# Attention over sampled blocks and an MLP on one core: one scale per pair of W_in pieces, block numbers read at once, zero rows on another queue, and another order of the work

## The chip, the cores and the metric

The kernel runs on one core of a Trainium2 chip. The metric is the device time of one execution in microseconds (us), and less is better. A core has the engines TensorE (PE in the profile, with its weight load as PEld), VectorE (DVE), ScalarE (ACT), GpSimd (POOL) and SyncE (SP). Each executes its own instructions in the order in which the program has them, and waits at an instruction until what it reads or overwrites is ready. DMA transfers are issued by an instruction on one of the engines (SPq and ACTq in the profile are the DMA-issuing instructions of SyncE and ScalarE) and then run beside it.

## The reference

```python
def _attn_ref(q, k, v, sampled_blocks):          # 4 batches, 8 heads, 768 positions, 64 wide
    scores = (1.0 / np.sqrt(D)) * np.matmul(q, k.transpose(0, 1, 3, 2))
    # mask: same or neighbouring block of 32; all rows and columns of the first and
    # the last block; and for each block of queries its 3 sampled blocks of keys
    scores = np.where(mask, scores, -1000000000.0)
    scores = scores - np.max(scores, axis=-1, keepdims=True)
    attn = np.exp(scores)
    attn = attn / (np.sum(attn, axis=-1, keepdims=True) + 1e-09)
    return np.matmul(attn, v).astype(np.float32)

def _moe_ref(x, w_in, w_out):                    # 3072 tokens, 512 -> 2048 -> 512
    h = x @ w_in
    sp = np.where(h > 20.0, h, np.log1p(np.exp(np.minimum(h, 20.0))))
    g = h * np.tanh(sp)
    return (g @ w_out).astype(np.float32)
```

The attention's output, with the heads side by side, is the MLP's input x. The two weights arrive with 64 bits to a number (8.4 MB each); everything else has 32.

## The kernel before, in words

**Number formats.** Each operand of a large product is scaled by a power of two and split into two f16 parts, a high one and the remainder, and a product is three f16 products. The scale comes from the sum of squares: a "gram" matmul of the operand with itself (L373), whose diagonal DVE adds up (L388, "diag"), a matmul with ones that adds over the partitions (L396), and three small DVE operations that make the power of two and its inverse (L407 to L409, "root").

**Weights.** W_in is worked on in 8 pieces of 256 columns (`piece_i`), W_out in 16 of 128 rows (`piece_o`). A piece is loaded into a buffer of its own kind (`wr`, of which there are 3, for W_in; `wor`, which shares the ring `raw` of 6 with q, k and v, for W_out), turned into f32 by three DVE operations (L901, L904, L907), and, for W_in, measured (gram, diag, root) and split: the high part on ACT (L962) or DVE (L964), the low part on DVE (L968). The scale of one piece of W_in is a column of `ws`; two pieces share a root, and four DVE instructions for each such pair, later than the root, make what the MLP needs of it: `scales_w` takes the larger of the two inverse scales (`gq`, L1033), its reciprocal (`rq`, L1034) and the factor `gsc` of each piece (L1035); `scales_b` then makes `hsc` (L1041). W_out has one scale in all.

**Attention.** Each batch is cut into 14 jobs (`attend`), here counted from 0. A job is a chain over the engines: scores S (L674, PE), maximum mx (L737, DVE), its negative nb (L746, ACT), the exponentials pt (L756, ACT), transposes t (L680, PE), the f16 high part ph (L779, ACT), the low part pl (for the first six jobs a product that subtracts, L787 on PE, and a copy, L792 on ACT; later L783 on DVE), the product with v into the tile obank (L818, PE), the division r and xs (L837 to L840, DVE), and transposes tx back into x, split into xh and xl (L864 to L873). The sampled keys are copied out of kt into kg, one block at a time, at an address that comes out of a register: on POOL (L611), or, for some of the early jobs, on ACT (L608), which reads the register with a `value_load` (L607) ahead of each copy. The rows of v are gathered by DMAs on SP's queue (L628 to L635, vg from vd); a duplicate among the sampled blocks reads rows of zeros behind each batch of vd, which four DMAs write at the program's start (`which`, L339 in the kernel after).

**MLP.** For each 256 tokens and each piece of W_in the h products (L1068, PE), the copy hs of a piece (L1079, ACT, scaled by gsc), the nonlinearity over a pair of pieces (L1098 to L1122), and the y products with W_out (L1162, and L1281 for the last tokens). The first 70 or so us are loads, scales and splits; from about 100 us on, the jobs of the attention and the MLP of the tokens already done run side by side.

**Order.** Every step is a task with a number, and the string `ORDER` gives the order in which the program has them. A letter behind a number puts the task on the second of its engines (for the loads of weights no letter is ACT and b is SP; for the high part of W_in no letter is ACT and b is DVE). `+n` puts n matmuls ahead of the task whose result nobody reads (`fill`, L1506, "fillers" below).

## Time and profile before

| what | value |
|---|---|
| time before, median of 3 runs | 738.99 us (736.54 to 740.02) |
| the profiled execution, its own time | 739.2 us |
| its span in the profile | 737.4 us |
| TensorE clock granted, mean over the span | 0.983 of full speed |
| PE busy | 695.9 us (94%) |
| DVE, ACT, POOL busy | 566.1, 583.0, 298.4 us |
| DMA, mean over the span | 140 GB/s |

The profiled execution's own time is 1.8 us more than its span, and 0.2 us more than the median of the runs. The profile's page cuts the span into 40 equal slices; PE is below nine tenths in the first six of them only, that is in the first 110 us.

### The profile page before, as it was taken

What the parts mean: (1) busy time and instruction counts of PE and PEld (TensorE: products, weight loads), DVE (VectorE), ACT (ScalarE), POOL (GpSimd) and SP (SyncE); (2) the same over time, 40 slices, a digit from 0 to 9 for tenths busy, and PEclk for the clock granted to TensorE, in tenths of its full rate; (3) what the DMA queues carried; (4) which work ended last, traced back from release to release, by engine and by line L of the source; (5) the groups of instructions that cost most, each with busy time, mean ns of one, the idle gap of its engine ahead of it and who ended that gap; (6) DMA issues with size and microseconds to landing.
All of it is one profiled execution on the core that took longest, in us unless ns stands there. A gap on an engine that the chain in (4) does not pass through costs nothing.

```text
span 737.4 us, 28793 instructions
## 1 busy us (share of the span) xinstructions
PE 695.9 (94%) x11758; PEld 532.9 (72%) x11758; DVE 566.1 (77%) x1139; ACT 583.0 (79%) x927; POOL 298.4 (40%) x390
## 2 busy tenths in 40 slices
PE   5667799999999999999999999999999999999997
PEld 3445588865776767776777767677776778888887
DVE  6998788898777766878868768898897685745584
ACT  3695588999987878888888889978777787777782
POOL 2120424518554463174852623674574631023101
PEclk9978899999999999999999999999999999999999
DMA  9886767652444653335336564353423563000001
GB/s 327 289 256 201 217 212 195 206 148 64 141 117 139 189 175 98 97 120 171 114 105 178 180 216 112 130 140 92 152 85 95 166 212 143 1 1 16 29 17 71
DMA packets 60041, 103.59 MB, mean 140 GB/s; under 512 B 8579, under 2 KB 20868, under 8 KB 59908
## 3 DMA queue, kind: packets, MB, share of 16 engines
q1 hardware_dynamic: 59568, 100.96, 44.3%
q8 instruction: 92, 1.51, 0.9%
q10 hardware_dynamic: 340, 0.79, 0.3%
q14 instruction: 41, 0.34, 0.1%
HBM read 84.58 MB, written 17.14 MB: 138 GB/s over the span
## 4 chain that ended last, share of the span: by engine, by line
PE 79%; DVE 8%; DMA 7%; ACT 2%; issue 1%; SPq 1%; ACTq 0%; DVEq 0%
PE h_None L1068 30%; PE y L1162 21%; PE yr L1281 9%; PE t L680 6%; PE obank L818 5%; PE s L674 5%; DMA wor<-in_moe_w_out_dram 2%; DMA raw_k<-in_k_dram 2%; DMA vg<-vd 2%; PE obank L1281 1%; PE tx L680 1%; DVE mx L737 1%; DVE wo L904 1%; DMA raw_v<-in_v_dram 1%; DVE pl L783 1%
## 5 line engine op out<-in xcount | busy, mean ns | idle before, releaser
L1068 PEld LDWEIGHTS <-wi 128*128 128x128 f16 x2304 | 223.7, 98 | 35.2 <-issue 1.6
L1068 PE MATMUL h_None<-xh,wi 128*128 128x256 f16 x1152 | 207.1, 273 | 0.0
L611 POOL COPY kg<-kt 128x256 f16 x246 | 115.5, 504 | 154.6 <-PE s L674 128.2
L1162 PE MATMUL y<-wo,g 128*128 128x512 f16 x672 | 160.6, 379 | 0.0
L1068 PE MATMUL h_None<-xl,wi 128*128 128x256 f16 x576 | 157.3, 273 | 0.4 <-DVE xl L867 0.4
L1162 PEld LDWEIGHTS <-g 128*128 128x128 f16 x768 | 73.5, 98 | 68.5 <-issue 0.6
L756 ACT ACTIVATE pt<-s,nb,ns 128x256 f32<-128x256 f32 (+1 forms) x208 | 106.9, 582 | 0.7
L1120 POOL TENSOR_TENSOR g<-hs_None,g 128x1024 f16<-128x1024 f32 x33 | 73.3, 2223 | 72.4 <-ACT g L1114 54.5
L783 DVE SCALAR_TENSOR_TENSOR pl<-t,ph 128x512 f16<-128x512 f32 x99 | 67.0, 685 | 31.2 <-ACT ph L779 30.8
L779 ACT ACTIVATE ph<-t 128x512 f16<-128x512 f32 x112 | 66.0, 598 | 30.9 <-PE t L680 30.5
L1079 ACT ACTIVATE hs_None<-h_None,gsc 128x512 f32<-128x512 f32 x96 | 65.6, 688 | 20.8 <-PE h_None L1068 18.4
L1107 DVE SCALAR_TENSOR_TENSOR hs_None<-us_None,hs_None 128x1024 f32<-128x1024 f32 x48 | 59.6, 1241 | 24.4 <-ACT us_None L1106 24.3
L680 PE MATMUL t<-ident,pt 128*128 128x128 f32 x448 | 69.1, 284 | 7.6 <-ACT pt L756 4.7
L1068 PE MATMUL h_None<-xr,wi 128*128 128x256 f16 x576 | 68.6, 273 | 0.0
L680 PEld LDWEIGHTS t<-ident,pt 128*128 128x128 f32 x448 | 54.7, 147 | 18.5 <-issue 5.6
L737 DVE TENSOR_REDUCE mx<-s 128x4 f32<-128x1024 f32 x44 | 53.6, 1219 | 16.0 <-PE s L674 15.8
L1098 ACT ACTIVATE us_None<-hs_None,hsc 128x1024 f32<-128x1024 f32 x48 | 55.2, 1149 | 4.1 <-DVE sg L1148 2.9
L1103 POOL TENSOR_TENSOR us_None<-us_None 128x1024 f32<-128x1024 f32 x16 | 33.0, 2062 | 54.7 <-DVE us_None L1101 48.8
L818 PEld LDWEIGHTS <-ph 128*32 128x32 f16 x2408 | 43.4, 97 | 14.7 <-issue 10.0
L1106 ACT ACTIVATE us_None<-us_None 128x1024 f32<-128x1024 f32 x48 | 50.7, 1058 | 0.3
L1105 ACT ACTIVATE us_None<-us_None 128x1024 f32<-128x1024 f32 x48 | 50.6, 1057 | 0.3
L818 PE MATMUL obank<-vg,ph 128*32 128x129 f16 (+2 forms) x2168 | 46.1, 211 | 3.4 <-DMA vg<-vd 3.2
(262 smaller groups left out, 1238.8 us busy)
## 6 DMA issues: line engine op xcount, KB each, us to landing
vg<-vd SPq DMA_DIRECT2D x320, 65.0 KB, 2.4
vg<-vd SPq DMA_DIRECT2D x80, 195.0 KB, 3.0
wr<-in_moe_w_in_dram SPq DMA_DIRECT2D x8, 1024.0 KB, 8.1
wor<-in_moe_w_out_dram SPq DMA_DIRECT2D x15, 512.0 KB, 4.5
vd<-v SPq DMA_DIRECT2D x12, 520.0 KB, 4.4
vg<-vd SPq DMA_DIRECT2D x12, 520.0 KB, 4.4
raw_k<-in_k_dram SPq DMA_DIRECT2D x12, 512.0 KB, 6.8
raw_q<-in_q_dram SPq DMA_DIRECT2D x12, 512.0 KB, 4.6
```

The source lines that it names most:

```text
L611: nc.gpsimd.tensor_copy(out=dst, in_=tl["kt", b][:, :, ds(j, BS)])
L680: nc.tensor.matmul(out, src, ident, start=start, stop=stop, is_transpose=True)
L737: nc.vector.tensor_reduce(out=mx.rearrange("p g w -> p (g w)"), in_=tl[ks].rearrange("p g (w k) -> p (g w) k", k=KT), axis=AX.X, op=ALU.max)
L756: ex = lambda o, x, g, w: nc.scalar.activation(out=o, in_=x, func=AF.Exp, bias=nb[:, g, w:w + 1], scale=tl["ns", b, sus[w]["qb"] // TB][:, ...
L779: nc.scalar.activation(out=new(at_, "ph", ("ph", i, j), [P, 2, 2, P], F16), in_=tl["t", i, j], func=AF.Copy, scale=PSC)
L783: nc.vector.scalar_tensor_tensor(out=new(at_, "pl", ("pl", i, j), [P, 2, 2, P], F16), in0=tl["t", i, j], scalar=PSC, in1=tl["ph", i, j], o ...
L818: nc.tensor.matmul(obank[cs, at:at + v1 - v0], p[:, k, g, cs], vt[:, k, 2 * c + g, v0:v1], start=j == 0 and g == 0 and k == 0 and n == 0, ...
L1068: nc.tensor.matmul(h[:, f2, 0:n].rearrange("p (s q) -> p s q", q=BS), wi[:, fp, w, cc, fs], x[:, s0:s0 + sn, cc], start=f2 == 0 and k == 0 ...
L1079: nc.scalar.activation(out=tl[kq][:, 2 * (fp % 2):2 * (fp % 2) + 2, 0:n], in_=tl[kh][:, :, 0:n], func=AF.Copy, scale=gsc[:, fp:fp + 1])
L1120: add("POOL", 2.3 * c, lambda: nc.gpsimd.tensor_tensor(out=g(1), in0=hs(), in1=g(0), op=ALU.subtract), r=[kq, ("gh",) + kp], w=[kp], use=[kg],
L1162: nc.tensor.matmul(tl[ky], tl["g", b, t, k][:, g, f, q], wo_at(fc)[:, w], start=fc == 0 and n == 0, stop=fc == NFC - 1 and n == 2)
L1281: nc.tensor.matmul(R(i), lhs, rhs, start=head and j == n == 0, stop=k == NFC // 4 - 1 and j == 1 and n == 2, skip_group_check=True)
```

## The change

Four things change.

- Two pieces of W_in that follow one another (a quad, four times 128 columns) get one scale. Their grams add into one PSUM tile, one diag and one root of a single column follow, and the root writes its inverse straight into `gq`. `scales_w` goes, and so do `iv_i`, `gsc` and `rq`; the copy hs is scaled by a constant.
- The block numbers of the gathers that ACT does are read into registers by one instruction at the program's start, behind the operations that make them, where before each of 18 was read by an instruction of its own ahead of its copy. 30 numbers are read; ACT has 21 of the copies now.
- The four DMAs that write the rows of zeros go to SP's queue, in a task of their own (`zero_rows`), where before ACT issued them right behind the memset.
- `ORDER` is another one. Among what moves: 42 fillers where there were 24, and at other places; 12 of the 24 loads of weights are issued by ACT (pieces 2, 4, 6 and 7 of W_in, and 8 of the 16 of W_out) where one was; the high parts of two pieces of W_in are made by DVE; the order of the small DVE operations.

```diff
-    iv_i = const.tile([P, NFP], F32, name="iv_i")
-    gsc, gq, rq, sco = (const.tile([P, n], F32, name=name) for n, name in ((NFP, "gsc"), (NFC // 4, "gq"), (NFC // 4, "rq"), (NFC // 4, "sco")))
+    gq, sco = (const.tile([P, NFC // 4], F32, name=name) for name in ("gq", "sco"))
...
+        tl["zeros"] = z
+        early.extend(su["qb"] * NR + r for job in jobs for su in job["sus"] if su["early"] and not job["dense"] for r in range(NR))
+        regs["act"] = nc.values_load_multi_w_load_instructions(
+            offk[0:1, early[0]:early[-1] + 1], [mybir.EngineType.Activation], min_val=0, max_val=S - BS,
+            skip_runtime_bounds_check_because="a sampled block is one of NB")[1]
+
+    def zero_rows():
         for b in range(B):
-            nc.scalar.dma_start(out=vd[b][S:S + BS].rearrange("s h d -> s (h d)"), in_=z)
-
+            nc.sync.dma_start(out=vd[b][S:S + BS].rearrange("s h d -> s (h d)"), in_=tl["zeros"])
...
-                    j = nc.scalar.value_load(offk[0:1, k:k + 1], min_val=0, max_val=S - BS)
+                    j = regs["act"][k - early[0]]
...
-        add_gram(("wi", k), [lambda: a0_i(k)], [key], "h", ss, [ks], [("wq", ks)] if k == k0 else (), cls)
...
-            add_root(kp, lambda: tl[ks], lambda: root(kp, new(sb, "ws", ksc, [P, 2]), iv_i[:, k0:k + 1]),
+            add_gram(("wi", k0), [lambda n=n: a0_i(n) for n in (k0, k)], [("wi", k0), key], "h",
+                     lambda: new(sb, "wq", ks, [P, 1]), [ks], [("wq", ks)], cls)
+            add_root(kp, lambda: tl[ks], lambda: root(kp, new(sb, "ws", ksc, [P, 1]), gq[:, k0 // 2:k0 // 2 + 1]),
                      [ks], [], [ksc, ("iv", k0)], [("ws", ksc)], cls)
...
-        sc = lambda: tl[("ws", k0)][:, k - k0:k - k0 + 1]
+        sc = lambda: tl[("ws", k0)]
...
-    def scales_w(k):
-        def fn():
-            nc.vector.tensor_reduce(out=gq[:, k:k + 1], in_=iv_i[:, 2 * k:2 * k + 2], axis=AX.X, op=ALU.max)
-            nc.vector.reciprocal(out=rq[:, k:k + 1], in_=gq[:, k:k + 1])
-            nc.vector.tensor_scalar(out=gsc[:, 2 * k:2 * k + 2], in0=iv_i[:, 2 * k:2 * k + 2], scalar1=rq[:, k:k + 1], scalar2=-2.0 * GSC, op0=ALU.mult, op1=ALU.mult)
-        add("DVE", 0.7, fn, r=[("iv", 2 * k)], w=[("gs", k)], key=-3)
...
-                                 scale=gsc[:, fp:fp + 1])
+                                 scale=-2.0 * GSC)
...
+    add("SP", 2.0, zero_rows, r=["off"], w=["z"], use=[("z",)], key=9, lat=2.5, kind=("dma", 1.2, B))
...
-    any(scales_w(k) for k in range(NFC // 4))
...
 ORDER = """
-    7 0 1 2 3 8+3 4 9 6 5 10 76 11 12 52 13 14 117b 18 93b 15 54 16 28+2 19 92 22 62 20 17 84 23 99b 29 24 68 67 30 21
+    7 0 1 2 3 5 4 6 9+3 10 115b 11 12 13+1 14 15 19 16 20 23 17 92 29+4 98b 21 18 62 24 30+1 25 80 73 31 22 54 74 26
```

Where a scale is made, DVE's rows change as follows, for the first two pieces of W_in (`wr` is a piece as it was loaded, `gram_wi` its gram, `tp_w` the root's tile). Before, from the diag of the one piece to the end of their common root:

```order
L388 SCALAR_TENSOR_TENSOR gram_wi_785,wq_851<-gram_wi_785,ident 128x128
L907 SCALAR_TENSOR_TENSOR wi<-wr_305,wi 128x1024
L737 TENSOR_REDUCE mx_984<-s_604 128x4
L901 TENSOR_SCALAR wi<-wr_585 128x1024
L837 TENSOR_SCALAR r_1018<-obank 128x2
L838 RECIPROCAL r_1018<-r_1018 128x2
L840 TENSOR_TENSOR xs_1019<-obank,r_1018 128x128
L388 SCALAR_TENSOR_TENSOR gram_wi_986,wq_851<-gram_wi_986,ident 128x128
L904 SCALAR_TENSOR_TENSOR wi<-wr_585,wi 128x1024
L407 TENSOR_SCALAR tp_w_1032<-tp_w_1032 128x2
L408 TENSOR_SCALAR iv_i<-tp_w_1032 128x2
L409 TENSOR_SCALAR ws_1050<-tp_w_1032 128x2
```

In the kernel after, from the last operation on piece 0 as loaded (`wr_383`), over the one diag for both pieces, to the root; `wr_597` is the next piece:

```order
L907 SCALAR_TENSOR_TENSOR wi<-wr_383,wi 128x1024
L737 TENSOR_REDUCE mx_796<-s_624 128x4
L907 SCALAR_TENSOR_TENSOR wi<-wr_305,wi 128x1024
L901 TENSOR_SCALAR wi<-wr_597 128x1024
L388 SCALAR_TENSOR_TENSOR gram_wi_800,wq_996<-gram_wi_800,ident 128x128
L904 SCALAR_TENSOR_TENSOR wi<-wr_597,wi 128x1024
L837 TENSOR_SCALAR r_1014<-obank 128x2
L838 RECIPROCAL r_1014<-r_1014 128x2
L840 TENSOR_TENSOR xs_1015<-obank,r_1014 128x128
L907 SCALAR_TENSOR_TENSOR wi<-wr_597,wi 128x1024
L407 TENSOR_SCALAR tp_w_1001<-tp_w_1001 128x1
L408 TENSOR_SCALAR gq<-tp_w_1001 128x1
```

One diag stands where two did, and the root is one column wide and writes `gq`. Behind these rows follow the root's last operation (L409), the high part of piece 0, now made by DVE (L964), and the first operation on piece 6 (L901), which is loaded into the buffer that the first of these rows gives free.

On DVE, ahead of the maximum of job 6 (`mx<-s`), with the last pieces of W_in and the first of W_out (`wor`) in work. Before:

```order
L901 TENSOR_SCALAR wo<-wor_2383 128x512
L968 SCALAR_TENSOR_TENSOR wi<-wi,ws_2245 128x1024
L901 TENSOR_SCALAR wo<-wor_2548 128x512
L904 SCALAR_TENSOR_TENSOR wo<-wor_2383,wo 128x512
L1041 TENSOR_SCALAR hsc<-gq,iv_x 128x1
L904 SCALAR_TENSOR_TENSOR wo<-wor_2548,wo 128x512
L737 TENSOR_REDUCE mx_2859<-s_2702 128x4
```

After:

```order
L840 TENSOR_TENSOR xs_2517<-obank,r_2516 128x256
L901 TENSOR_SCALAR wo<-wor_2271 128x512
L1041 TENSOR_SCALAR hsc<-gq,iv_x 128x1
L904 SCALAR_TENSOR_TENSOR wo<-wor_2271,wo 128x512
L907 SCALAR_TENSOR_TENSOR wo<-wor_1511,wo 128x512
L968 SCALAR_TENSOR_TENSOR wi<-wi,ws_2136 128x1024
L1041 TENSOR_SCALAR hsc<-gq,iv_x 128x1
L737 TENSOR_REDUCE mx_2689<-s_2562 128x4
```

Before, the decode of two pieces of W_out is begun in the stretch ahead of the maximum (two L901); after, of one.

On ACT, around the small operation nb of the same job, with the low parts pl of the job before it. Before:

```order
L779 ACTIVATE ph_1_2853<-t_1_2803 128x512
L746 ACTIVATE nb_2876<-mx_2859,ns_1_1282 128x4
L792 ACTIVATE pl_0_2878<-t_0_2644 128x512
L792 ACTIVATE pl_1_2880<-t_1_2803 128x512
L756 ACTIVATE pt_2930<-s_2702,nb_2876,ns_1_1282 128x256 x4
```

After:

```order
L779 ACTIVATE ph_1_2691<-t_1_2664 128x512
L792 ACTIVATE pl_0_2693<-t_0_2521 128x512
L962 ACTIVATE wi<-wi,ws_2049 128x1024
L746 ACTIVATE nb_2711<-mx_2689,ns_1_1284 128x4
L792 ACTIVATE pl_1_2761<-t_1_2664 128x512
```

Both low parts of the earlier job stand behind nb before; after, the first of them stands ahead of it.

## Rows read from the trace of the kernel before

**Rows 1.** Busy time by stretch: us, PE, PEld, DVE, ACT, POOL, PEclk, DMA share, GB/s.

```profile
0.00:20.00 20.00, 10.81 (x92) 7.98 (x100) 11.97 (x43) 7.48 (x9) 6.50 (x19) 1.00 0.94 332
20.00:70.00 50.00, 32.56 (x955) 24.39 (x939) 47.78 (x91) 37.21 (x74) 7.22 (x11) 0.86 0.80 246
70.00:100.00 30.00, 23.67 (x640) 18.78 (x639) 22.49 (x51) 17.34 (x34) 9.97 (x16) 0.83 0.69 207
...
140.00:700.00 560.00, 557.10 (x8858) 418.87 (x8856) 421.73 (x849) 465.37 (x733) 254.44 (x329) 1.00 0.40 123
```

**Rows 2.** DVE's groups, 15 to 130 us, shapes apart: busy us, mean ns, idle before.

```profile
L904 DVE SCALAR_TENSOR_TENSOR wo<-wor,wo 128x512 int32<-128x512 int32 x13 | 11.3, 883 | 0.0
...
L907 DVE SCALAR_TENSOR_TENSOR wo<-wor,wo 128x512 int32<-128x512 int32 x13 | 9.3, 721 | 0.0
L968 DVE SCALAR_TENSOR_TENSOR wi<-wi,ws 128x1024 f16<-128x1024 f32 x7 | 8.9, 1276 | 0.0
L904 DVE SCALAR_TENSOR_TENSOR wi<-wr,wi 128x1024 int32<-128x1024 int32 x7 | 8.5, 1220 | 0.0
...
L901 DVE TENSOR_SCALAR wo<-wor 128x512 int32<-128x512 int32 x15 | 6.8, 456 | 4.5 <-DMA wor<-in_moe_w_out_dram 4.5
...
L901 DVE TENSOR_SCALAR wi<-wr 128x1024 int32<-128x1024 int32 x7 | 5.0, 714 | 0.4 <-DMA wr<-in_moe_w_in_dram 0.4
...
L840 DVE TENSOR_TENSOR xs<-obank,r 128x256 f32<-128x256 f32 x8 | 3.4, 425 | 0.3
L1035 DVE TENSOR_SCALAR gsc<-iv_i,rq 128x2 f32<-128x2 f32 x4 | 2.8, 699 | 0.1
...
L388 DVE SCALAR_TENSOR_TENSOR gram_wi<-gram_wi,ident 128x128 f32<-128x128 f32 x8 | 2.3, 290 | 0.0
...
L1034 DVE RECIPROCAL rq<-gq 128x1 f32<-128x1 f32 x4 | 0.7, 164 | 0.1
...
L1033 DVE TENSOR_REDUCE gq<-iv_i 128x1 f32<-128x2 f32 x4 | 0.6, 144 | 0.0
```

**Rows 3.** DVE's timeline between the maxima of jobs 5 and 6.

```profile
77.73 1.23 DVE L737 TENSOR_REDUCE mx<-s 128x4 f32<-128x1024 f32 x1 [1.47 <-PE s L674]
78.87 0.15 DVE L1033 TENSOR_REDUCE gq<-iv_i 128x1 f32<-128x2 f32 x1
...
80.90 0.15 DVE L1033 TENSOR_REDUCE gq<-iv_i 128x1 f32<-128x2 f32 x1
...
86.30 0.45 DVE L901 TENSOR_SCALAR wo<-wor 128x512 int32<-128x512 int32 x1 [2.04 <-DMA wor<-in_moe_w_out_dram]
...
90.00 1.21 DVE L737 TENSOR_REDUCE mx<-s 128x4 f32<-128x1024 f32 x1
```

**Rows 4.** ACT's timeline around nb of job 6.

```profile
91.25 0.30 ACT L746 ACTIVATE nb<-mx,ns 128x4 f32<-128x4 f32 x1 [4.83 <-DVE mx L737]
91.46 1.06 ACT L792 ACTIVATE pl<-t 128x512 f16<-128x512 f32 x2
```

**Rows 5.** PE's timeline: three fillers, and the next product of job 5 with v.

```profile
58.48 0.81 PE L1506 MATMUL obank<-neg 128*128 128x240 f16 x3
...
92.09 0.25 PE L818 MATMUL obank<-vg,pl 128*32 128x65 f16 x4 [3.18 <-ACT pl L792]
```

**Rows 6.** SP's timeline, 86 to 93 us: start, us until issued.

```profile
86.73 5.77 SPq L893 DMA_DIRECT2D wor<-in_moe_w_out_dram  x3
92.70 0.33 SPq L628 DMA_DIRECT2D vg<-vd  x1
```

**Rows 7.** DMA issues by group: KB each, median us from issue to landing.

```profile
wr<-in_moe_w_in_dram SPq DMA_DIRECT2D x8, 1024.0 KB, 8.1
...
vd<-z ACTq DMA_DIRECT2D x4, 65.0 KB, 5.5
```

**Rows 8.** Waits of all engines: us in total, times, longest.

```profile
ACT kg L608 <- issue: 2.9, 9, 0.9
```

**Rows 9.** Issues at L893: ns min/median/max, first and last start us.

```profile
L893 SPq DMA_DIRECT2D wor<-in_moe_w_out_dram x15: 327/382/1650, 50.4 to 127.8; - x15
```

More of the change, by code (lines that the diff above doesn't have):

```diff
@@ L572, in globals_v @@
         add("SP", 0.9, fn, r=VD3(b), w=[("vg", n)], key=-1, lat=2.3, kind=("dma", 0.5, 2))
-    regs = {}
+    regs, early = {}, []
     def block_at(eng, name, table, k, hi):
@@ L1013, in fn @@
             nc.vector.tensor_tensor(out=gox, in0=gmx, in1=iv_o, op=ALU.mult)
-        add_root(kp, lambda: tl["am", "wo"], fn, [("am", "wo")], [("gs", k) for k in range(NFC // 4)], ["sc_o"], (), cls - 2)
+        add_root(kp, lambda: tl["am", "wo"], fn, [("am", "wo")], [("iv", k) for k in range(0, NFP, 2)], ["sc_o"], (), cls - 2)
     def parts_o(fc, cls):
@@ L1042, in scales_b @@
                 out=hsc[:, b, ks], in0=gq[:, ks], scalar1=iv_x[:, b:b + 1], scalar2=-0.5 * float(2.0 ** -26) / GSC,
-                op0=ALU.mult, op1=ALU.mult), r=[("gs", k) for k in ks] + [("sc", "v", b, 0)], w=[("hsc", b, k)], key=-3)
+                op0=ALU.mult, op1=ALU.mult), r=[("iv", 2 * k) for k in ks] + [("sc", "v", b, 0)], w=[("hsc", b, k)], key=-3)
         add("DVE", 0.2, lambda: nc.vector.tensor_scalar(
@@ L1079, in hs_fn @@
             nc.scalar.activation(out=tl[kq][:, 2 * (fp % 2):2 * (fp % 2) + 2, 0:n], in_=tl[kh][:, :, 0:n], func=AF.Copy,
-                                 scale=gsc[:, fp:fp + 1])
-        add("ACT", 0.72 if part is None else 0.45, hs_fn, r=[kh, ("gs", fp // 2)], w=[("hsw", b, t, fp, part)],
+                                 scale=-2.0 * GSC)
+        add("ACT", 0.72 if part is None else 0.45, hs_fn, r=[kh], w=[("hsw", b, t, fp, part)],
             new=[("hs", kq)] if fp % 2 == 0 else (), use=[kq], key=-4)
@@ L1380, in attn_mish_kernel @@
         load(0, "v", [j], "us" if j < 2 else "hs")
-    add("ACT", 1.0, lambda: which(new), w=["off", "z"],
-        new=[("hs", ("z",))], key=-9, lat=6.0, kind=("dma", 0.9, 2 + B))
+    add("ACT", 1.0, lambda: which(new), w=["off"],
+        new=[("hs", ("z",))], key=-9, lat=6.0, kind=("dma", 0.9, 2))
+    add("SP", 2.0, zero_rows, r=["off"], w=["z"], use=[("z",)], key=9, lat=2.5, kind=("dma", 1.2, B))
     for j in T3:
@@ L1665 @@
[L1665 to L1667 removed]
+    7 0 1 2 3 5 4 6 9+3 10 115b 11 12 13+1 14 15 19 16 20 23 17 92 29+4 98b 21 18 62 24 30+1 25 80 73 31 22 54 74 26
+    94b 58 28 32 81 33 116 163 198b 56 27 34 52 39 35 43 40 196 188 164 75 36 60 68 117 165 166 37 167 118 38 70 176
@@ new lines @@
+    1512 2218 1479 1513 1528 1460 2231 1489 1480 1531 1514 1515 2236 2167 1461 2200b 1497 2333 1481 2232 1482 1516
+    1532 2237 2201 1529 1620 2334 2202 2229 2233 2203 1534 2335 1501 1579 2238 2336b 1483 1517 1530 1502 2230 1518
+    2239 1535 1520 2254 2219 2337 1536 1521 2327 2240 1537 2255 1511 2220 1519 2204b 1522 2234 1538 1578 1503 1508
+    2259 1504 2205 2241b 1505 1542 2242 2235 1576 1543 1575 1539 1544 2260 1540 2221 1541 2250 2243 2256 1553 2244
+    2222 1523 1554 2251 1533 1524 1555 2275 2252b 1556 2247 2276 1550 1557 2257 2223 1561 2226 1581 1562 2261 1545
@@ L1668 @@
+    2676 2642b 2679 2643 2674 2678 2685 2644 2681 2645b 2682 2690 2692b 2673 2686 2688 2693 2689 2695 2680 2696 2683
+    2697 2699 2698 2687 2691 2694 2700 2701
 """
```

201 lines of the change are left out of this document (95 added, 106 removed), and 17 rows, old and new, of the table ORDER.

## The prediction, made before the kernel ran

> **What bounds the kernel now.** I read first the busy time by stretch, since the change works on the weights and the first jobs only [rows 1]. From 140 to 700 us PE is busy for 557.1 of 560 us, at full clock; there the kernel waits for nothing but PE's own work, which the change leaves as it is. What PE loses it loses early: it is idle for 9.2 us of the first 20, for 17.4 of the 50 that follow, and for 6.3 between 70 and 100, together 32.9 us. A time saved here moves the whole rest forward, if PE gets its work sooner by it.
>
> Next I ask which engine sets the pace in each of these stretches. Between 20 and 70 us it is DVE, with 47.78 of 50 us busy, where ACT has 37.21 and POOL 7.22 [rows 1]. So what DVE is spared there counts nearly whole, and what another engine is spared counts nothing. Between 70 and 100 us no engine is full (DVE 22.49 of 30), so the timelines of the engines have to tell. They show one large hole, and a chain of waits through four engines. DVE begins the maximum of job 5 at 77.73 and that of job 6 only at 90.00, 12.27 us later, with 2.04 us of waiting for a load of W_out in between [rows 3]. ACT stands 4.83 us at nb of job 6 for that maximum, and the two low parts pl of job 5, which need nothing of it, stand behind nb in ACT's order [rows 4]. PE waits 3.18 us for the first of them at 92.09 [rows 5]. On SP three loads of W_out take 5.77 us to issue, from 86.73, and a gather of v stands behind them until 92.70 [rows 6]; 15 loads there have a median of 0.382 us, so three of them without a wait are 1.15, and 4.6 us are a wait for buffers [rows 9].
>
> **The change, part by part.** The sum is made against the profiled execution's own time, 739.2 us, which is 0.2 above the median of the three runs.
>
> *The scale.* Four of eight diags go, at 0.29 us each: 1.2 us. The twelve instructions of the four scale groups go: 0.6, 0.7 and 2.8 us, together 4.1 [rows 2]. I count half of these groups, 2.05 us, in DVE's full stretch, and leave the other half to the next part, since two of the groups begin, with L1033, between the two maxima [rows 3]. Against that, DVE takes over the high parts of two pieces of W_in from ACT. The trace has no such operation on DVE. The nearest rows are the first step of the decode, one input of the same 128x1024 (0.714), and the low part, two inputs and the same output (1.276) [rows 2]; I take the first, as it too is a scalar operation on one input, and get 1.4 for both, 2.55 at most. So DVE's full stretch gets 1.2 + 2.05 - 1.4 = 1.85 us shorter. The bounds: 3.9 if all four groups lay in it (1.2 + 4.1 - 1.4), and 0.6 if the high parts take 2.55 and the factor's operation L1035, whose 0.699 is far above the 0.164 of its neighbour L1034 of a like size [rows 2], had mostly been a wait: the groups are then 12 x 0.16 = 1.9, half of it 0.95, and 1.2 + 0.95 - 2.55 is even -0.4. I keep +0.4 us as the worst end.
>
> *The order between the maxima.* After the change DVE has between the two maxima, by the rows' means: the maximum 1.22 [rows 3], twice 0.456 and 0.883 and 0.721 for the decode of W_out, a diag 0.29, a low part 1.276, an xs 0.425, and about ten small operations of 0.17: 9.0 us, with no second load of W_out to wait for [rows 2]. So job 6 gets its maximum 3.3 us earlier than the 12.27 of before, and pl of job 5 no longer waits for it, since the first stands ahead of nb. What PE gains by that is its own wait there, 3.18 us [rows 5]; I take 3.2, and 0 as the other end, where PE then waits for the next thing (the gather of v behind SP's loads, or job 6 itself).
>
> *The buffers of W_in.* There are three, so piece 6 is loaded into the one that the last operation on piece 0 frees. A load takes 8.1 us from issue to landing [rows 7], and its issue 0.38 [rows 9]: 8.5. From that operation to the first on piece 6, DVE has by the new order four operations of 1.22 (a maximum, two last steps of a decode, taken at the middle step's time, and one middle step), two of 0.71, a diag of 0.29, an xs of at most 0.43 and five small ones of 0.16: 7.8 us [rows 2, 3]. So where before DVE waited 0.4 us for W_in in all [rows 2], it now waits 0.7 for this piece; 0 if a few of those operations are held up themselves, 1.4 if piece 7 comes as late.
>
> *Edits that I cost at nothing.* The 18 reads of a register on ACT: the profile's row for what they left before a copy is 2.9 us in nine gaps [rows 8], and ACT has 12.8 us to spare in the 50 where DVE has 2.2 [rows 1]; if that cover is gone, they are worth the 2.9. Twelve loads issued by ACT instead of one cost it 11 x 0.38 = 4.2 us [rows 9], under the same cover. The zero rows: 0.26 MB leave the first 20 us, in which the transfers run at 332 GB/s with the engines 0.94 busy [rows 1, 7]; that is 0.8 us of transfer, which may bring what comes behind forward by as much, or nothing if the loads wait for DVE anyway; the four issues take SP 4 x 0.38 = 1.5 us at about 30 us [rows 9], and the first gathers of v stand behind them. I take nothing for both, with -0.8 and +1.5 as ends. The 18 more fillers take 0.27 us each (0.81 for three [rows 5]), 4.9 in all; PE has 32.9 us of idle time in the first 100 us, where they stand [rows 1], so nothing.
>
> The sum: 739.2 - 1.85 - 3.2 + 0.7 = 734.85, say **734.8 us**, by 4.4 us or 0.6% faster. All good ends together (3.9, 3.2, 0 for the buffers, 0.8, 2.9) give 728.4; all bad ends (+0.4, 0, +1.4, +1.5) give 742.5.
>
> One rule of the Trainium skill speaks against half of this. Much of the second part hangs on loads of W_out that come in time, and the row is SP's 5.77 us for three issues, with a gather behind them [rows 6]. The page "DMA: Bandwidth & Descriptors", section "Issuing engines are not separate DMA queues", says that DMAs started by different engines share the same transfer engines, and that starting them from several engines saves only the time that it takes to start them. By the row the gain is the gather's 4.6 us of standing in line; by the rule the loads themselves land no sooner for being issued on ACT.
>
> **The rivals.** *The loads still come late* (about the same time). The mechanism is the one just told: DVE's 2.04 us of waiting for W_out [rows 3] stays, wherever it then stands, and the part between the maxima brings 3.2 - 2.0 = 1.2. The sum is then 739.2 - 1.85 - 1.2 + 0.7 = **736.9**. For it speaks that 70 to 100 us moves 207 GB/s with a DMA share of 0.69, below the 332 of the start, so that it is not the transfer alone that limits [rows 1], but a buffer; against it that the gather no longer stands behind.
>
> *The gain is hidden*: PE's holes are filled by another wait of the same length, since each job's chain passes DVE and ACT in turn, and the 1.85 of DVE's are given back to W_in pieces (1.4 of 1.85). The time is 739.2 - 0.5 - 0 = **738.7**.
>
> *The clock* (faster still). PE's granted clock is 0.86 between 20 and 70 us and 0.83 between 70 and 100, and 1.00 before and from 140 us on [rows 1]; with its two levels, 2.4 and 1.2 GHz, that is 0.28 x 50 + 0.34 x 30 = 24 us at half. More fillers at other places could end this. If the 10 us at half in the second stretch went, where PE is busy for 0.79 of the time, PE would be spared 10 x 0.79 / 2 = 4.0 us, and the time is **730.8**. Against it: there PE waits for others, and its steps are a part of the chain only. The page "TensorE: Matmul & The Clock Gate", Part 1, says that the clock is throttled by default and that activity of the engine releases it; these rows agree, with 1.00 in the stretch where PE is over 0.9 busy, though the first 20 us have it too, with PE busy for 10.81.
>
> *ACT stands in its own way* (slower). ACT now issues eight loads of W_out into the ring of six that q, k and v share. An issue that finds no free buffer holds up every operation behind it: nb, pt, ph, and with them DVE and PE. The price of one such wait is what SP's row shows, 4.6 us [rows 6, 9]. One of them on the chain makes the gain nothing (734.8 + 4.6 = 739.4); the case is slower than before by 0.5% from 8.1 us of such waits on; two of them give 734.8 + 9.2 = **744.0**. For it speaks that ACT is the engine through which each job's chain passes three times; against it that SP waited there in a stretch where ACT had 12.7 us free, so that a well placed issue costs nothing [rows 1].
>
> **How the numbers follow.** The sum as worked out: 0.41. The clock besides: 0.10. Loads late: 0.21. Gain hidden: 0.14. ACT blocked: 0.14. A difference of 0.5%, 3.7 us, is about what a measurement of this kernel can tell from none, so faster is below 735.3 and slower above 742.7. The sum's own range, 732 to 737, lies on both sides of 735.3; I count three fifths of it, 0.25, as surely faster, half of the rest (0.08) too, and with the clock and a part of the late loads (0.07, as the other terms may be at their good ends) that makes 0.50. ACT blocked gives 0.12 slower, the rest of it the same; what is left, 0.38, is the same. The predicted time is 734.8; the range is 728.4 to 742.5, the ends of the bounds, with the slower rival outside.
>
> **What would show it.** Right: no L1033 to L1035 on DVE, four diags; PE idle between 20 and 70 us down from 17.4 by about 2 and between 70 and 100 from 6.3 to about 3; 140 us to the end unchanged; the wait of nb of job 6 below 2 us. Wrong: DVE rows that wait for wr by more than 2 us; ACT's issues L893 of over 1 us with PE or DVE waiting for ACT behind them; the high parts L964 over 1.3 us; PE's granted clock at 0.95 or more before 100 us, which would be the clock's rival; or PE idle in the steady part, where I expect nothing.

## The result, and the profile after

The changed kernel takes 746.44 us (median of 4 runs, 745.63 to 747.72) where the kernel before took 739.44 (4 runs). The ratio is 1.0118, with a 95% interval from 1.0084 to 1.0152: it is slower, by 1.2%, which is 8.7 us by the ratio (the medians alone are 7.0 apart), and outside of the range forecast. The profiled execution took 745.63, its span is 743.9.

The busy time by stretch has the columns of [rows 1]:

```profile
0.00:20.00 20.00, 11.50 (x119) 8.57 (x119) 12.21 (x44) 7.64 (x10) 6.79 (x19) 0.95 0.95 328
20.00:70.00 50.00, 28.55 (x662) 21.10 (x647) 37.82 (x61) 26.10 (x56) 4.47 (x5) 0.64 0.76 230
70.00:100.00 30.00, 26.11 (x822) 20.33 (x821) 26.32 (x61) 22.45 (x48) 11.99 (x17) 0.95 0.82 233
...
140.00:700.00 560.00, 553.25 (x8822) 414.62 (x8820) 435.48 (x866) 449.57 (x722) 246.58 (x313) 1.00 0.41 123
700.00:743.90 43.90, 40.04 (x367) 35.58 (x364) 26.72 (x41) 26.56 (x29) 10.80 (x8) 1.00 0.08 31
```

Against [rows 1], three numbers stand out. Between 20 and 70 us every engine does less: DVE is busy for 37.82 us instead of 47.78, ACT for 26.10 instead of 37.21, PE for 28.55 instead of 32.56. None of them is full any more, so they wait for one another. PE's granted clock is 0.64 there instead of 0.86 (that the clock is not the cause is shown below, at the two halves of the order). And PE is idle for 6.75 us between 140 and 700 us, where it was idle for 2.90. Only the stretch from 70 to 100 us went as forecast: PE is idle for 3.9 us instead of 6.3.

What stops the engines is in ACT's timeline of the changed kernel. An ACTq row is the issue of a load, and the wait in brackets is printed at the operation behind it:

```profile
34.89 0.40 ACTq L893 DMA_DIRECT2D wr<-in_moe_w_in_dram  x1
35.34 0.60 ACT L792 ACTIVATE pl<-t 128x512 f16<-128x512 f32 x1 [3.78 <-DMA vd<-z]
35.84 0.29 ACT L746 ACTIVATE nb<-mx,ns 128x4 f32<-128x4 f32 x1
...
48.62 0.37 ACTq L893 DMA_DIRECT2D wr<-in_moe_w_in_dram  x1
49.11 1.02 ACT L608 ACTIVATE kg<-kt 128x256 f16 x3 [6.07 <-DMA vg<-vd]
...
55.46 0.37 ACTq L893 DMA_DIRECT2D wr<-in_moe_w_in_dram  x1
55.88 0.30 ACT L746 ACTIVATE nb<-mx,ns 128x4 f32<-128x4 f32 x1 [3.47 <-DMA vg<-vd]
```

Three times ACT comes to a load of W_in, cannot issue it, and everything behind stands: 3.78, 6.07 and 3.47 us, 13.3 in all. The releaser is neither PE nor DVE, and not the buffer either. It is a transfer that has nothing to do with W_in, issued by SP: a gather of v for the second and the third, and for the first, by the profile, a zero row. The program shows why. DMAs signal their end by one of eight semaphores, DMAHW0 to DMAHW7, in turn, and an issue waits for the earlier one that had its own. These are the first and the second of the three in ACT's order, with what each waits for:

```
29 L893 DMA wr_798<-in_moe_w_in_dram 128x4x512 [waits DMAHW3_49,DMAHW0_49,DVE_49]
42 L893 DMA wr_1093<-in_moe_w_in_dram 128x4x512 [waits DMAHW6_49,DMAHW5_49,DVE_49]
```

Of the two semaphores of the first, DMAHW3 is that of the load that filled the buffer before (piece 0), and DMAHW0 is its own. Its own had last gone to the third store of v, and not to a zero row: the four zero rows have DMAHW1 to DMAHW4. On SP the stores stand right ahead of the zero rows:

```profile
24.23 7.92 SPq L553 DMA_DIRECT2D vd<-v  x3
32.20 2.24 SPq L339 DMA_DIRECT2D vd<-z  x4
```

The third store is issued at 31.8; the trace's semaphore signals have its last one at 34.83, 0.06 us ahead of ACT's issue at 34.89, and the last ones of the four zero rows at 35.05 to 35.76, behind it. So the name of the releaser in the profile's row is wrong here, and the store of v is what ACT waited for. For the second and the third, the last signals of their semaphores come at 48.55 and 55.36, and are those of gathers of v.

DVE is the buffer's last reader, and had been done: its last operation on the buffer of the first, the first row below, ended at 32.29, 2.6 us ahead of the issue. So ACT's work was tied to SP's transfers. (ACT's load of piece 2 at 25.32, ahead of the three, is another matter: it waited 1.23 us for its buffer, until DVE's last operation on piece 3.) DVE's timeline shows what follows:

```profile
31.07 1.22 DVE L907 SCALAR_TENSOR_TENSOR wi<-wr,wi 128x1024 int32<-128x1024 int32 x1
32.21 1.22 DVE L737 TENSOR_REDUCE mx<-s 128x4 f32<-128x1024 f32 x1
...
51.95 0.30 DVE L388 SCALAR_TENSOR_TENSOR gram_q<-gram_q,ident 128x128 f32<-128x128 f32 x1 [5.46 <-PE gram_q L373]
...
53.69 1.21 DVE L737 TENSOR_REDUCE mx<-s 128x4 f32<-128x1024 f32 x1
...
83.50 1.21 DVE L737 TENSOR_REDUCE mx<-s 128x4 f32<-128x1024 f32 x1
...
92.43 1.22 DVE L737 TENSOR_REDUCE mx<-s 128x4 f32<-128x1024 f32 x1 [0.73 <-PE s L674]
```

DVE's wait of 5.46 us leads back to ACT: the gram for which it waits stands in PE's order behind scores that wait for the copies kg of ACT's second stop (49.11 above).

```profile
50.18 0.34 PE L674 MATMUL s<-kg,q 64*32 64x160 f16 x8 [4.19 <-ACT kg L608]
```

The maxima of jobs 1 and 2 in DVE's timeline of the kernel before:

```profile
34.45 1.22 DVE L737 TENSOR_REDUCE mx<-s 128x4 f32<-128x1024 f32 x1
...
43.23 1.22 DVE L737 TENSOR_REDUCE mx<-s 128x4 f32<-128x1024 f32 x1
```

That of job 1 comes at 32.21 now, 2.2 us earlier. That of job 2 comes at 53.69, 10.5 us later; by job 6 it is 2.4 us later (92.43 for 90.00). From job 5 to job 6 it is 83.50 to 92.43, 8.9 us, where I had worked out 9.0 and the kernel before took 12.27 [rows 3].

### The profile page after: what moved, and what is told of

The parts are those of the page before. It is cut to its first block, busy times and chain, and to the rows that moved or that the text cites. A ratio compares the mean times of both kernels' runs of the same rounds, so it can differ in the third digit from the quotient of the medians.

```text
span 743.9 us, 28756 instructions
## 1 busy us (share of the span) xinstructions
PE 698.3 (94%) x11780; PEld 533.7 (72%) x11780; DVE 576.3 (77%) x1132; ACT 569.2 (77%) x924; POOL 296.5 (40%) x380
## 4 chain that ended last, share of the span: by engine, by line
PE 83%; DVE 9%; DMA 4%; issue 2%; SPq 2%; ACT 1%; ACTq 0%; DVEq 0%
PE h_None L1068 31%; PE y L1162 22%; PE yr L1281 8%; PE t L680 6%; PE s L674 5%; PE obank L818 5%; DMA vg<-vd 2%; PE tx L680 1%; PE obank L1281 1%; DMA wr<-in_moe_w_in_dram 1%; DMA raw_k<-in_k_dram 1%; DVE mx L737 1%; DVE wo L904 1%; SPq L580 1%; DVE wo L907 1%
## 5 line engine op out<-in xcount | busy, mean ns | idle before, releaser
L611 POOL COPY kg<-kt 128x256 f16 x243 | 111.8, 493 | 162.7 <-PE s L674 151.3
L1120 POOL TENSOR_TENSOR g<-hs_None,g 128x1024 f16<-128x1024 f32 x37 | 81.8, 2214 | 91.9 <-ACT g L1114 43.1
L1079 ACT ACTIVATE hs_None<-h_None 128x512 f32<-128x512 f32 x96 | 56.7, 594 | 23.5 <-PE h_None L1068 22.4
L1107 DVE SCALAR_TENSOR_TENSOR hs_None<-us_None,hs_None 128x1024 f32<-128x1024 f32 x48 | 63.3, 1319 | 8.2 <-ACT us_None L1106 8.2
L1103 POOL TENSOR_TENSOR us_None<-us_None 128x1024 f32<-128x1024 f32 x18 | 37.1, 2065 | 74.9 <-DVE us_None L1101 70.6
L674 PEld LDWEIGHTS <-q 64*32 64x32 f16 x2976 | 34.2, 94 | 22.3 <-issue 18.1
```

The costliest lines, as they stand in the source:

```text
L611: nc.gpsimd.tensor_copy(out=dst, in_=tl["kt", b][:, :, ds(j, BS)])
L674: nc.tensor.matmul(s[g][i * BS:(i + 1) * BS, c0 + cs.start:c0 + cs.stop], q[gs, c * NPR + i, qs], src[gs, a * NPR + i, ks], start=first an ...
L1107: add("DVE", 1.32 * c, lambda: nc.vector.scalar_tensor_tensor(out=hs(), in0=us(), scalar=-0.5, in1=hs(), op0=ALU.add, op1=ALU.mult), r=[ku ...
L1120: add("POOL", 2.3 * c, lambda: nc.gpsimd.tensor_tensor(out=g(1), in0=hs(), in1=g(0), op=ALU.subtract), r=[kq, ("gh",) + kp], w=[kp], use=[kg],
```

## The experiments

The runs of the kernel before that stand beside them have medians of 738.3 to 738.5 us. A difference in us is worked out from the ratios and 738.5, if nothing else is said; differences of the medians can be 1 us or so away from it.

**The loads back on SP.** All twelve loads that ACT issues, by the letter b:

```diff
-... 111 ... 145 ... 128 ... 149 ...        (pieces 2, 6, 4, 7 of W_in; W_out likewise)
+... 111b ... 145b ... 128b ... 149b ...
```

> The changed kernel with all twelve loads of weights that ACT issues put back on SP's queue, at the same places of the order. Theory A (ACT is held up): three issues of W_in loads on ACT wait 3.8, 6.1 and 3.5 us, in the trace of the changed kernel, for the end of another transfer on SP's queue, and pl, kg and nb stand behind them; without them the first jobs come earlier, PE idle between 20 and 70 us falls from 21.5 to 17 or less, and the time falls by 4 to 7 us, to 739.5 to 742.5. Theory B (the loads wait for buffers or for the transfers, whoever issues them): DVE then waits for W_in instead, and the time stays at 744 to 748.

743.59 us, 1.0093 (1.0060 to 1.0126, 4 runs). The three waits of ACT are gone and PE is idle for 16.5 us between 20 and 70, as theory A said; the time fell by 1.8 us only (2.9 by the medians), short of the 4 that it asked for, and the interval overlaps that of the changed kernel. A part of what theory B said is there as well: DVE, which waits for no load of W_in between 20 and 70 us in the changed kernel, now waits 2.78 us for the one that SP issues behind the zero rows. PE stayed idle for 6.85 us between 140 and 700.

**The code without the order.** The three edits with the order of before; `zero_rows` behind the third store of v.

> The three edits of the code (one scale per pair of pieces, one register load, zero rows on SP's queue behind the third store of v) with the order of before. Theory A: the edits do no harm, the order does; DVE is spared 1 to 4 us in its full stretch and the time is 735.5 to 739. Theory C (one scale makes both pieces of a pair wait for the later one, and the zero rows hold up SP): 741 or more.

740.27 us, 1.0030 (1.0003 to 1.0056). Neither theory as it stood: the edits do not gain, and cost little. The trace has one wait that is new, on SP and then on DVE. SP's timeline:

```profile
30.48 3.26 SPq L339 DMA_DIRECT2D vd<-z  x4
34.48 0.40 SPq L893 DMA_DIRECT2D wr<-in_moe_w_in_dram  x1
```

and DVE's:

```profile
42.26 0.69 DVE L901 TENSOR_SCALAR wi<-wr 128x1024 int32<-128x1024 int32 x1 [3.08 <-DMA wr<-in_moe_w_in_dram]
```

The same load and the same wait in SP's and DVE's timelines of the kernel before:

```profile
32.08 0.38 SPq L893 DMA_DIRECT2D wr<-in_moe_w_in_dram  x1
```

```profile
40.08 0.69 DVE L901 TENSOR_SCALAR wi<-wr 128x1024 int32<-128x1024 int32 x1 [0.41 <-DMA wr<-in_moe_w_in_dram]
```

The four zero rows keep SP for 3.26 us; the load of W_in behind them is issued at 34.48 instead of 32.08, and DVE waits 3.08 us for it instead of 0.41.

**The two halves of the order.** The code of after with the orders joined at the maximum of job 9.

```diff
-ORDER = after
+ORDER = after up to the maximum of job 9, then what is left in the order of before
```

> The code of after, with its order up to the maximum of job 9 (some 120 us) and the order of before from there on. Theory A with a second part (the later order loses 3.9 us by itself, as PE is idle for 6.75 us between 140 and 700 us where it was 2.90): 742 to 743.5. Theory D (all of the loss comes from the first 120 us, and the later gaps follow from it): 745 to 747.

748.61 us, 1.0156 (1.0125 to 1.0187).

> The code of after, with the order of before up to the maximum of job 9 and the order of after from there on. Theory A with its second part: the time of the code alone plus about 3.9, 740 to 743. Theory D: the same as the code alone, 736 to 739.

740.51 us, 1.0028 (0.9999 to 1.0057). The first lies above both ranges. The second lies in the range that I had written for theory A, 740 to 743, but that was meant as the time of the code alone plus 3.9; the code alone took 740.27, and this run the same, which is theory D. So the second part that I had given theory A falls: the later order costs nothing that can be measured, all is lost by what stands in the first 120 us. That PE is idle for 6.65 us between 140 and 700 in the first of the two, with the later order of before, says that those gaps as well are set by the early part. How an early part can do that was open here.

The first of the two also settles a rival, that the lower clock made the changed kernel slow. Its granted clock is 0.86 between 20 and 70 us, as in the kernel before, where the changed kernel had 0.64, and its profiled execution takes 748.06.

**The scale and the register load, without the zero rows' move.**

```diff
-    add("SP", 2.0, zero_rows, ...)
+            nc.scalar.dma_start(out=vd[b][S:S + BS]..., in_=z)      # in which(), as before
```

> The code with one scale and one register load, in the order of before, and with the zero rows issued by ACT at the start as before. In the run with all three edits SP took 3.26 us for the four zero-row issues, the fourth load of W_in behind them was issued at 34.48 instead of 32.08, and DVE waited 3.08 us for it instead of 0.41. Theory Z (the zero rows on SP cost what the scale spares): the wait goes back to about 0.4 and the time is 736 to 738. Theory Y (the scale gains nothing by itself, as DVE's time is not what sets the first jobs): 739 to 741, like the run with all three edits.

740.66 us, 1.0012 (0.9986 to 1.0039): theory Y by its time. DVE's wait for the fourth load is 1.54 us, over half of the way back to 0.41, and the trace has a cause that neither theory had. The scale of k is there at 11.09, by DVE's timeline,

```profile
10.94 0.15 DVE L407 TENSOR_SCALAR sc_k<-tp_k 128x1 int32<-128x1 int32 x1
```

and ACT takes it up at 11.85 only, by its own:

```profile
11.85 3.23 ACT L498 ACTIVATE kt<-raw_k,sc_k 128x1024 f16<-128x1024 f32 x3 [9.82 <-DMA raw_v<-in_v_dram]
```

In the changed kernel and the runs that have the register load and the zero rows on SP it begins at 10.25 to 10.61, and its wait ends with its scale. So the one register load delays nothing only when the zero rows do not stand ahead of it on ACT; with them, ACT begins 0.8 us late here.

**The zero rows alone**, in the kernel before.

```diff
-            nc.scalar.dma_start(out=vd[b][S:S + BS]..., in_=z)
+            nc.sync.dma_start(out=vd[b][S:S + BS]..., in_=tl["zeros"])
...
+    add("SP", 2.0, zero_rows, r=["off"], w=["z"], ...)
```

> The kernel before with one edit alone: the zero rows issued by SP behind the third store of v. Theory Z: DVE's wait for the fourth load of W_in grows to about 3 us and the time is 2 to 3 us longer, 740.5 to 742. Theory Y: 738 to 739.5.

740.19 us, 1.0027 (1.0000 to 1.0054), and DVE's wait is 2.67 us. The wait is that of theory Z; the time, 2.0 us longer, is at the low end of what it said, and the interval just touches none. With the scale and the register load besides, it was 1.0030: these two gave nothing back.

**The zero rows back on ACT**, in the changed kernel.

```diff
-            nc.sync.dma_start(out=vd[b][S:S + BS]..., in_=tl["zeros"])
+            nc.scalar.dma_start(out=vd[b][S:S + BS]..., in_=z)
```

> The changed kernel with the zero rows issued by ACT at the start again. In the changed kernel the second of ACT's W_in loads (piece 6) stands 3.78 us for a zero-row transfer. Theory A (ACT is held up by transfers on SP's queue): that wait shrinks, the two behind it (6.07 and 3.47, for gathers of v) may stay or move; the time falls by 1 to 4 us, to 742.5 to 745.5. Theory B (the loads wait for buffers): 746 to 748.

747.16 us, 1.0111 (1.0071 to 1.0150): no gain, and by the number theory B. ACT's waits are now 1.22, 4.33 and 6.04 us, 11.6 in all instead of 13.3. The first of them is for DVE, the last reader of the buffer, as theory B said; the other two are for gathers of v. The expectation rested on the profile's name for the releaser: the 3.78 us had been for the third store of v, and what moved the wait is that the semaphores go to the DMAs in turn, so that the load of piece 6 now shares one with the first store. And the run has a loss of its own, since the register load stands behind the zero rows on ACT again: ACT takes up the scale of k at 12.01, 1.28 us after it is there. So this run does not decide between the theories; the next one does.

**The four loads of W_in alone back on SP.**

```diff
-... 111 ... 145 ... 128 ... 149 ...        (pieces 2, 6, 4, 7 of W_in; W_out stays)
+... 111b ... 145b ... 128b ... 149b ...
```

> The changed kernel with the four loads of W_in alone put back on SP's queue; the eight loads of W_out stay on ACT. Theory A: the three waits of ACT go, and the time is that of the run with all twelve loads on SP, 742 to 745. The rival (the W_out loads on ACT are what holds up): 746 to 748.

742.86 us, 1.0053 (1.0030 to 1.0076), 4.8 us less than the changed kernel (3.6 by the medians), with an interval clear of its own. The three waits are gone. These four loads are the largest cause. The eight of W_out are not free of such waits: in this run two of them stand for a gather of v, by ACT's timeline,

```profile
60.84 0.36 ACTq L893 DMA_DIRECT2D wor<-in_moe_w_out_dram  x1
61.25 0.60 ACT L779 ACTIVATE ph<-t 128x512 f16<-128x512 f32 x1 [3.13 <-DMA vg<-vd]
...
81.62 0.33 ACTq L893 DMA_DIRECT2D wor<-in_moe_w_out_dram  x1
82.00 0.60 ACT L792 ACTIVATE pl<-t 128x512 f16<-128x512 f32 x1 [3.50 <-DMA vg<-vd]
```

but moving them to SP as well (1.0093, the run with all twelve there) was no faster.

**Fewer fillers besides.** 22 of them left out of that kernel.

```diff
-153+8 ... 119+4 ... 405+4 ... 346+3 ... 355+3
+153 ... 119 ... 405 ... 346 ... 355
```

> The changed kernel with the four loads of W_in on SP's queue and 22 of its 46 fillers left out, so that it has as many as the kernel before. With the loads on SP alone it stood at 1.0053 of before, and PE was idle for 6.8 us between 140 and 700 us where the kernel before was for 2.9; five of the gaps there lie right behind a 16 KB transfer of PE's own instructions, one in the kernel before. Theory F (44 more PE instructions shift where each stretch of instructions ends, and PE waits for the next one at other places): the gaps go with the fillers, PE is idle for 3 to 4.5 us there, and the time is 1.000 to 1.003 of before. Theory G (the rest of the loss is the order's, and the fillers helped the clock): 1.005 or more.

741.65 us, 1.0046 (1.0022 to 1.0071). The waits of PE between 140 and 700 us (total, times, longest) are, with 46 fillers in the run ahead of this one,

```profile
PE obank L818 <- DMA vg<-vd: 2.0, 1, 2.0
PE h_None L1068 <- issue: 1.9, 2, 1.1
PE obank L818 <- issue: 1.4, 1, 1.4
```

and with 24

```profile
PE obank L818 <- DMA vg<-vd: 3.3, 1, 3.3
PE t L680 <- DVE pl L783: 0.7, 1, 0.7
```

All that PE spent waiting on "issue", that is for nothing that the profile shows, went with the fillers, as theory F said. A wait for a gather of v grew by 1.3 us, so that PE is idle for 4.64 us there (6.76 with 46), just above the 4.5 of theory F, and the median fell by 1.2 us, within the intervals and short of its 1.003. The trace is clear here, the time is not.

**More fillers in the kernel before**, 22 at places where PE waits anyway:

```diff
-8+3 ... 32 ... 175
+8+5 ... 32+8 ... 175+12
```

> The kernel before with 22 fillers more and nothing else, put where PE waits anyway: 2 at the start, 8 ahead of the first v root (2.45 us of waiting there) and 12 ahead of the first transposes (3.92 us). Theory F: the gaps behind instruction transfers come up here too, PE is idle for 5 us or more between 140 and 700 us, and the time is 2 to 4 us longer, 1.003 to 1.005. The clock (the rival that I priced at 4.0 us): granted clock between 20 and 70 us over 0.95 and the time 2 to 4 us shorter. Neither: no change.

741.02 us, 1.0034 (1.0014 to 1.0054), with PE idle for 6.13 us between 140 and 700: theory F, and no gain by the clock (0.80 between 20 and 70 us). The waits on issue came up in this kernel too, by the same view:

```profile
PE obank L818 <- issue: 3.1, 3, 1.8
PE obank L818 <- DMA vg<-vd: 1.1, 1, 1.1
PE h_None L1068 <- issue: 0.6, 1, 0.6
```

In the kernel before the view begins with the one such wait there:

```profile
PE obank L818 <- issue: 1.8, 1, 1.8
```

In the traces of all these runs each wait on issue of over 0.8 us between 140 and 700 us begins within 2 us of the start of a 16 KB transfer on queue 8, the one of the profile's instruction queues that has 92 transfers in a span, before as after. That these bring PE's instructions is what the shift by fillers speaks for; the trace does not name them.

**My second term by itself.** The maximum of job 6, and one pl of job 5, moved forward in the order of before:

```diff
-232 ... 451 ... 452 434 438          (first step on a W_out piece; mx 6; nb 6, pl, pl of job 5)
+451 232 ... 434 452 438
```

> The kernel before with its order changed in two places: the maximum of job 6 ahead of the first step on the W_out piece for which DVE waits 2.04 us, and the first low part pl of job 5 ahead of nb of job 6. It is the second term of my sum by itself, 3.2 us. If it holds: PE's wait of 3.18 us at 92 us goes, 735 to 737, 0.995 to 0.997. Theory H (the first 100 us have slack: PE's wait there is paid back by later waits): no change, 0.998 to 1.002.

736.93 us, 0.9988 (0.9965 to 1.0012). The trace did all that was wanted: the maximum is at 84.97 instead of 90.00 in DVE's timeline, and pl and nb follow on ACT without the 4.83 us of waiting:

```profile
84.97 1.22 DVE L737 TENSOR_REDUCE mx<-s 128x4 f32<-128x1024 f32 x1 [0.82 <-PE s L674]
```

```profile
86.08 0.59 ACT L792 ACTIVATE pl<-t 128x512 f16<-128x512 f32 x1
86.55 0.30 ACT L746 ACTIVATE nb<-mx,ns 128x4 f32<-128x4 f32 x1
```

PE is idle for 2.9 us between 70 and 100 instead of 6.3. The time fell by 0.9 us by the ratio, which is theory H's range, with an interval that takes in no change and 2.6 us: less came through than the 3.2 that PE was spared. Some of it came back at once, as PE waits 2.3 us for gathers of v in that stretch where it waited 1.1 before.

**The mirror image.** The kernel before with four loads of W_in on ACT:

```diff
-... 111b ... 147b ... 129b ... 153b ...    (pieces 2, 6, 4, 7 of W_in)
+... 111 ... 147 ... 129 ... 153 ...
```

> The kernel before with four loads of W_in (the fourth, fifth, seventh and eighth) issued by ACT at the same places of the order, and nothing else. Theory A: each stands in ACT's order for a transfer of SP's queue or for a buffer, in all 8 us or more of waits ahead of pl, kg or nb in ACT's rows between 25 and 60 us, and the time is 3 to 6 us longer, 1.004 to 1.008. The rival (ACT has 12.8 us to spare there, so its waits cost nothing): 0.999 to 1.002.

740.97 us, 1.0036 (1.0008 to 1.0064), 2.7 us slower: theory A in the other kernel, just below the range that it said; the interval excludes no change, but reaches into the rival's range. There is one long wait here rather than three, of 5.63 us, for a gather of v, less than the 8 us that it asked for:

```profile
45.32 0.41 ACTq L893 DMA_DIRECT2D wr<-in_moe_w_in_dram  x1
45.78 1.02 ACT L756 ACTIVATE pt<-s,nb,ns 128x256 f32<-128x256 f32 x2 [5.63 <-DMA vg<-vd]
```

**The scale alone**, in the kernel before.

```diff
-    def scales_w(k):
...
-                                 scale=gsc[:, fp:fp + 1])
+                                 scale=-2.0 * GSC)
```

> The kernel before with one edit alone, one scale per pair of W_in pieces; the zero rows and the reads of block numbers as before. In the run with the scale and the register load, ACT began to convert k at 11.85, 0.76 us after its scale was there, and a low part on DVE took 3.07 us beside an operation of POOL, in the place where L1035 had taken 1.74. Theory P (L1035's time was mostly a wait for POOL, which the next operation takes over; the register load costs the other 0.8 us): conversion of k right behind its scale, DVE's long operation at some 55 us again, and a gain of 0 to 1.5 us: 0.998 to 1.000. Theory of my first term (1.85 us at 20 to 70 us, and what the other two groups bring): 0.995 to 0.997.

739.29 us, 1.0008 (0.9979 to 1.0037): no gain that can be measured, which is nearest to theory P. As that theory said, k is taken up right behind its scale (11.19 and 11.16), and the long operation is there again. Where L1035 took 1.74 us in the kernel before, beside an operation of POOL (DVE's and POOL's timelines of the kernel before),

```profile
53.85 1.74 DVE L1035 TENSOR_SCALAR gsc<-iv_i,rq 128x2 f32<-128x2 f32 x1
```

```profile
53.44 2.12 POOL L535 TENSOR_TENSOR q<-raw_q,q 128x1024 f16<-128x1024 f32 x1
```

a low part takes 3.23 instead of its usual 1.28 without it (the same two timelines of this run):

```profile
54.59 3.23 DVE L962 SCALAR_TENSOR_TENSOR wi<-wi,ws 128x1024 f16<-128x1024 f32 x1
```

```profile
54.62 2.12 POOL L529 TENSOR_TENSOR q<-raw_q,q 128x1024 f16<-128x1024 f32 x1
```

Both end only after POOL's operation has ended (55.56 and 56.74). Most of the time of L1035 was a wait for POOL, and taking the instruction away gave the wait to the next one. The page "SBUF — State Buffer", section "Who interferes with whom", of the Trainium skill says that VectorE and GpSimd share a pair of ports and that this pair is an exclusive lock; these rows agree.

**The three causes out at once**: the changed order with W_in's loads on SP, 24 fillers, the zero rows and the reads of block numbers as before.

```diff
-                    j = regs["act"][k - early[0]]
+                    j = nc.scalar.value_load(offk[0:1, k:k + 1], min_val=0, max_val=S - BS)
...
-... 111 ... 145 ... 128 ... 149 ... 153+8 ...
+... 111b ... 145b ... 128b ... 149b ... 153 ...
```

> The changed kernel's order with the three causes taken out at once: the four loads of W_in on SP's queue, the zero rows issued by ACT at the start as before, 24 fillers instead of 46; the block numbers are read one by one as before, so that the register load does not stand behind the zero rows. If the causes are the whole of the loss of 1.2%: 0.998 to 1.002. If something else in the order costs as well: 1.003 or more.

739.83 us, 1.0022 (0.9995 to 1.0050). So the three causes, with the reads of block numbers, account for 0.96 of the 1.18 per cent; whether the 0.22 that is left is anything, these runs don't tell. (The numbers in the edit are those of the changed kernel's order.)

**Both gains together**: the scale, and the maximum of job 6 moved.

```diff
-    def scales_w(k):
...
-(first step on a W_out piece) ... (mx 6) ... (nb 6) (pl of job 5)
+(mx 6) (first step on a W_out piece) ... (pl of job 5) (nb 6)
```

> One scale per pair, in the order of before with the maximum of job 6 and one low part of job 5 moved forward (the run with that alone stood at 0.9988, with an interval from 0.9965 to 1.0012), all else as before. If the two gains add up: 0.995 to 0.998, the fastest of all. If each only moves a wait: 0.999 to 1.001.

736.48 us, 0.9978 (0.9959 to 0.9997): the fastest of all, and faster than the kernel before, though by 0.2% only. Its interval overlaps that of the run with the maximum alone, and the scale alone gained nothing, so that the scale adds anything here is not shown.

## Why the prediction was wrong

**The step that failed** is the one on the edits that I costed at nothing, in its sentence on the loads: "Twelve loads issued by ACT instead of one cost it 11 x 0.38 = 4.2 us", and that "under the same cover", the 12.8 us that ACT had to spare. The time that an issue takes was right (0.33 to 0.41 us). But spare time covers work, and not a wait in the middle of an order: what stands behind the issue was late, and other engines waited for it. What the runs showed in its place: three of the issues waited 13.3 us for DMAs of SP that had their semaphores. The wait was there to be read without any run, since a program names the semaphores on which an instruction waits. Four loads cost 4.8 us in the changed order and 2.7 in that of before.

**The rival that came nearest** is that ACT stands in its own way. Its engine and its sign were right, and that the operations of the jobs' chains stand behind it (it named nb, pt and ph; they were pl, kg and nb); its place was not (the loads of W_in, not the eight of W_out) nor its mechanism (a semaphore that SP's transfers use too, not a buffer), and with 13.3 us of waits in place of 9.2 it was priced too low: 744.0 instead of 746.4. I gave it 0.14, because SP had waited in a stretch where ACT had time; that was an argument about busy time again.

**The zero rows** I gave 1.5 us as their worst end. They took 3.26 us of SP in the order of before (2.24 in the changed one), not 1.5, and cost 2.0 in the kernel before (1.0027, none to 4.0). In the changed kernel DVE has no wait for the load behind them; with W_in's loads back on SP it has one of 2.19 us, or of 2.78 where those of W_out are on SP as well. So their cost there seems to be hidden under ACT's waits, which no run measures by itself.

**The fillers** I costed at nothing, since they lie in PE's waits. There they did lie (and there are 46 of them, not the 42 that I had counted). What they cost comes 100 to 400 us later: they move the places at which PE waits on issue, close to the 16 KB transfers, and 22 of them cost 0.34% in the kernel before.

**The reads of block numbers** I costed at nothing, with 2.9 us as the good end. They brought nothing that can be measured: the three edits together took 1.0030, the zero rows alone 1.0027.

**The buffers of W_in**, +0.7 us, came out at the good end of that term: DVE has no wait for W_in between 20 and 70 us in the changed kernel. That is no sign that the sum was right, as DVE itself came later.

**The first term**, 1.85 us from DVE, brought nothing that can be measured (1.0008). DVE was spared the work: between 20 and 70 us it is busy for 45.45 us instead of 47.78 with the scale alone. The bound that I named, that L1035 "had mostly been a wait", holds for the longest of the four, 1.74 us, and the wait stayed. The high parts on DVE were right: 0.75 us for 0.714.

**The second term**, 3.2 us, was right in its mechanism (8.9 us between the maxima for 9.0; PE's wait of 3.18 gone), though the near match of 8.9 and 9.0 is in part luck: 1.1 us of the 8.9 are waits that the sum did not have, and the work took 1.2 less than by the rows' means. It was mis-sized: 0.9 us by itself (0.9988, none to 2.6), and 1.6 with the scale (0.9978). A longer wait for gathers of v, 2.3 us for 1.1, took a part of the rest; what took the remainder is open.

**The clock** went the other way between 20 and 70 us: 0.64 for 0.86, and fillers did not raise it in the kernel before either (0.80). Between 70 and 100 us, the stretch for which I had priced the rival at 4.0 us, it did rise, to 0.95 from 0.83, and the kernel was slower all the same. The first half of the order with 0.86 between 20 and 70 us was no faster either, so the clock doesn't account for the loss.

## What to carry to other kernels

An issue of a DMA is an instruction like any other in its engine's order, and in a program that hands out its completion semaphores in turn, as this one, it waits for the earlier DMA that had the same one. Before moving loads to an engine through which a chain passes, look at what each issue waits for, not only at how long it takes or how idle the engine is. The releaser that a profile names is inferred; where the argument hangs on it, the program's own waits decide. An instruction that takes far longer than its like can be a wait with another name, as L1035 was here, and removing it then gains nothing; what an engine is spared counts when a run has shown where the engine's next wait ends.

## What was not expected of the hardware

PE waits for 0.8 to 2.4 us close to some of the 92 transfers of one instruction queue, and with 22 fillers more or fewer it waits at other ones, or at none. And ACT's copy of h became shorter by having a constant for a scale instead of a column. From the views by source line of the kernel before and of the changed kernel (min, median and max in ns):

```profile
L1079 ACT ACTIVATE hs_None<-h_None,gsc x96: 664/687/727, 95.2 to 714.0; 128x512 f32<-128x512 f32 x96
```

```profile
L1079 ACT ACTIVATE hs_None<-h_None x96: 574/595/640, 95.8 to 721.1; 128x512 f32<-128x512 f32 x96
```

That is 92 ns for each, 8.8 us of ACT's time in 96 of them. I had not priced it. The run with the scale alone has it too, and gained nothing (1.0008): in the steady part PE is busy nearly throughout. The page "ScalarE: Activation LUTs", section "What ACT_TABLE_LOAD costs", of the Trainium skill gives about 93 ns for each operand that is a column, and these rows agree.
